# Shorter tile choice on VectorE, two small steps moved to POOL and ACT, unbroken moves of the probabilities and a new issue order, in a fused attention and top-1 mixture-of-experts kernel

## The chip, the core and the metric

The kernel runs on one core of a Trainium2 chip. The metric is the device time of one execution in microseconds (us). PE is TensorE, DVE is VectorE, ACT is ScalarE, POOL is GpSimd, and SP is the engine whose queue issues most DMAs.

## The reference

Four batches of 12288 queries of width 128 attend to 768 pooled keys, which serve as values too. Each of the 49152 resulting rows then goes through the one expert (of eight) that its logits favour.

```python
kv_pool = kv.reshape(B, H // r, r, W // r, r, C).mean(axis=(2, 4))
k = v = kv_pool.reshape(B, -1, C) @ w_sr
s = scale * (q @ k.transpose(0, 2, 1))
a = np.exp(s - s.max(-1, keepdims=True))
a /= a.sum(-1, keepdims=True) + 1e-09
x = (a @ v).reshape(B * S, D)
logits = x @ w_gate
expert_idx = np.argmax(logits, axis=1)
probs = np.exp(logits - logits.max(-1, keepdims=True))
probs /= probs.sum(-1, keepdims=True) + 1e-09
gate_w = probs[np.arange(N), expert_idx]
out[mask] = gate_w[mask, None] * (np.maximum(x[mask] @ w1[e], 0.0) @ w2[e])
```

## The kernel before

The queries are cut into 96 blocks of 512 rows (four groups g of 128), and one block is one round of a software pipeline. A value is kept as a high part in the matmul's own format and a low part that is the rest, so that each product takes three matmuls (`mm3`, L229 to L232: high by high, high weight by low data, low weight by high data). ACT makes the high part with a copy (`high`, L215) and DVE or POOL subtracts it to get the low part (`low`, L218).

One round holds pieces of several blocks at different stages. For the block that is in attention: `turn_q`, `high_q` and `low_q` turn and split the queries (`ql` is subtracted on POOL); `scores` are 24 matmuls of 128x384; `maxima` (L341, DVE) and `exps` (L349, ACT) make the probabilities; `turn_p` (L358, DVE) turns them in blocks of 32x32 into `pb`; `move_p` (L368) brings the blocks to their partitions in `pt` with 16 DMAs from SP's queue; `high_p` and `low_p` split `pt` into `pth` (ACT) and `pt` (POOL), in three pieces n; `values` are 18 matmuls; `copy_x` copies the result out. `route` follows. `turn_x` (L484) multiplies by the identity and the gate's weights at once; DVE makes logits, the one-hot `oh` and its counts `tot`; `gate` ends in L555, and `norm_row` (L502, ACT, four instructions) scales the rows by it into `row`; `ranks` (L559, L560) are two small matmuls that count rows; `places` adds positions up (DVE, then POOL, L570 and L571); `put` (L579) scatters the rows to the expert's list `xs` in DRAM with four indirect DMAs that POOL issues. `row` also gets a token number and padding, which POOL writes (L470, L471) for a later block.

For the tile of 512 rows that is in an expert: `choose` (L639) picks the tile's expert in small DVE steps of width 8 that run one behind the other; `weights` fetches new weights; `read` loads the rows as `xb`; `turn_m`, `high_m` and `low_m` make `xt`, `xh` and `xl` (`xl` is subtracted on DVE); `first` and `second` are 48 matmuls of 128x512, with `hh` (L808, ACT) and `hlow` (L812, DVE) between them; `copy_y` (L830, ACT) takes the sum out as `yt`, `turn_y` (L835, PE) turns it, `rows_y` (L841, ACT) copies it, and `put` (L846) scatters it to the output with four indirect DMAs of POOL.

PSUM has eight banks. Three of them go round in a list (`take` takes the oldest free one, `give` returns it): `first`, `ranks`, `turn_y` and the second part of `turn_x` take theirs from it, so a taker waits for whoever last read the bank. The first six blocks turn their probabilities with PE and move nothing.

The order of PE, ACT and DVE is written out by hand: each step is put at a time of a plan, in units of which a round has 16, and the table `AT` holds these times. Each engine runs its steps in the order of those times and waits at a step until its inputs are there. POOL's and SP's orders are made by the scheduler of the language.

Of the kernel before, what the change touches and what calls it, by code (L numbers as in the profile page):

```python
# [10 lines left out]
F32 = mybir.dt.float32  # L11
F32R = mybir.dt.float32r
# [4 lines left out]
ALU = mybir.AluOpType  # L17
# [4 lines left out]
P = 128  # L22
# [10 lines left out]
    "turn_q": -0.15, "high_q": 3.96, "low_q": 4.25, "maxima": 1.13, "exps": 2.45, ("first_p", 0): 6.32,  # L33
    ("first_p", 1): 4.1, ("first_p", 2): 5.9, ("first_p", 3): 5.1, ("first_p", 4): 5.32,
    ("first_p", 5): 7.4, "first_high": 0.5, "first_low": 1.3, "first_values": 2.0, "turn_p": 2.65,
    "move_p": 16.3, ("high_p", 0): 26.62, ("high_p", 1): 28.22, ("high_p", 2): 29.02, "low_p": 0.8,
    ("values", 0): 37.6, ("values", 1): 38.01, ("values", 2): 39.41, ("values", 3): 40.11,
    ("values", 4): 41.61, ("values", 5): 42.21, "copy_x": 0.6, "turn_x": 1.76, "logits": 0.8, "row": 0.9,
    "gate_exp": 2.27, "gate": 2.29, "ranks": 1.12, "places": 1.21, "put_x": 3.7, "expert": 24.43,
    "fetch": -11.4, "read": -9.0, "weights": -5.41, ("cut", 0, 0): -5.5, ("cut", 1, 0): 3.67,  # L40
    ("cut", 0, 1): 1.39, ("cut", 1, 1): 3.0, "turn_m": -4.26, "high_m": 0.26, "low_m": 2.94, "first": 4.65,
    "high_h": 0.0, "low_h": 1.35, "second": 4.85, "copy_y": 0.42, "turn_y": 1.5, "rows_y": 4.66,
# [20 lines left out]
def tile_pooled_attention_top1_moe(ctx: ExitStack, tc, q, kv, w_sr, w_gate, w1, w2, out):  # L63
# [150 lines left out]
    def high(dst, src):  # L214
        nc.scalar.copy(out=dst, in_=src)  # L215
# [95 lines left out]
    def attention(t, i):  # L311
# [43 lines left out]
        def turn_p(g):  # L355
            if g == 0:
                own["pb"] = ap.tile([P, NK // SQ, G, SQ], F32, name="pb")
            nc.vector.transpose(  # L358
                out=own["pb"][:, :, g, :], in_=own["prob", g].rearrange("p (k t) -> p k t", t=SQ)
            )  # L360

        def move_p():
            pt = own["pt"] = ap.tile([P, NB, T], F32R, name="pt")
            src = own["pb"].rearrange("p (k c) g t -> p c k (g t)", c=QT)
            dst = pt.bitcast(F32).rearrange("p k (a t) -> p a k t", a=QT)
            for a in range(QT):
                for c in range(QT):
                    nc.sync.dma_start(  # L368
                        out=dst[c * SQ : (c + 1) * SQ, a], in_=src[a * SQ : (a + 1) * SQ, c]
                    )  # L370

        def high_p(n):
            own["pth", n] = ap.tile([P, 2, T], F32R, name="pth", bufs=4)
            high(own["pth", n], own["pt"][:, 2 * n : 2 * n + 2].bitcast(F32))

        def low_p(n):
            v = own["pt"][:, 2 * n : 2 * n + 2]
            low(v, v.bitcast(F32), own["pth", n], nc.gpsimd)


        def turn_first(n):
            if n == 0:
                own["pt"] = ap.tile([P, NB, T], F32R, name="pt").rearrange("p n t -> p (n t)")
                own["pb"] = ap.tile([P, NK // SQ, G, SQ], F32, name="pb").rearrange("p n g t -> p (n g t)").bitcast(F32R)
# [15 lines left out]
        def values(k):  # L400
# [3 lines left out]
            if i < FIRST:  # L404
                ph, pl = (own[x].rearrange("p (g b t) -> p g b t", g=G, b=NB)[:, :, k, :] for x in ("pt", "pb"))
            else:
                ph, pl = own["pth", k // 2][:, k % 2], own["pt"][:, k]
# [52 lines left out]
    state["rows"] = count0  # L460
    state["puts"] = []

    def route(t, i, own):
        def norm():
            sums = own["sum"] = table("sum", G, 3)
            nc.vector.tensor_scalar_add(sums, own["sums"], 1e-9)
# [78 lines left out]
        def gate(n):  # L545
            if n == 0:
                own["se"] = rp.tile([P, G], F32, name="se")
# [66 lines left out]

    order = table("order", E, 1)
# [4 lines left out]
    def prefer(tag, last, held, base):  # L620
# [3 lines left out]
            out=pri, in0=last, scalar=float(E), in1=wdesc, op0=ALU.mult, op1=ALU.add  # L624
# [14 lines left out]
    def choose(j):  # L639
# [46 lines left out]
        with nc.allow_low_precision("row numbers below 2**24 are exact"):  # L686
            nc.vector.reduce_sum(out=num, in_=pks, axis=AX.X)
        state["some"] = some
# [4 lines left out]
            out=nheld, in0=state["held"][j % 2], scalar=none, in1=pick, op0=ALU.mult, op1=ALU.add  # L693
# [74 lines left out]
    def experts(t, j):  # L768
# [133 lines left out]
    nc.vector.tensor_copy(out=more, in_=state["some"])  # L902
# [31 lines left out]
```

## Time and profile before

| what | value |
|---|---|
| time, median of 3 runs | 2428.05 us (2422.09 to 2429.71) |
| profiled execution, its own time | 2419.68 us |
| profiled execution, its span | 2417.9 us |
| PE busy | 2166.5 us (90%) |
| DVE busy | 1873.8 us (77%) |
| POOL busy | 1706.7 us (71%) |
| ACT busy | 1469.0 us (61%) |
| mean share of 16 DMA engines, from 300 to 2150 us | 0.65 |

The profiled execution is one run with the profiler on; its time is its span and 1.8 us around it, and it lies 8.4 us under the median of the runs. Busy shares are averages over a filling stage, a long steady stage and a draining stage. PE's busy time counts overlapping matmuls once, and their ends are modelled. In a row of waits the first name is who waited, the second is whose work ended the wait.

### The profile page before, as it was taken

The page shows a single profiled execution, that of the slowest core. Times are in us where ns is not written, and L with a number is a line of the kernel's source. Part 1 is how long each engine was busy: PE and PEld are TensorE (multiplying, and loading weights), DVE is VectorE, ACT ScalarE, POOL GpSimd, SP SyncE. Part 2 cuts the span into 40 slices and gives each one's busy share as a digit, 9 for nine tenths or more (in the row PEclk, how much of TensorE's full clock was granted, in tenths as well). Part 3 has the DMA queues.
Part 4 walks back from the last instruction along what each step waited for, and adds up shares of the span by engine and source line. Part 5 has one row for each costly group of instructions (what it writes and reads, how often), then busy time and mean ns, then how long its engine had stood idle before and what let it go on. Part 6 is the DMA issues. An engine that isn't in the chain of part 4 may idle for free.

```text
span 2417.9 us, 41081 instructions
## 1 busy us (share of the span) xinstructions
PE 2166.5 (90%) x10444; PEld 1803.9 (75%) x10444; DVE 1873.8 (77%) x4883; ACT 1469.0 (61%) x2935; POOL 1706.7 (71%) x1855
## 2 busy tenths in 40 slices
PE   4779999999999999999998999999998999999875
PEld 3667777787777777778777777777777777778665
DVE  6566879988777788988777788997877778788564
ACT  2656666666666666666665666666665666666443
POOL 2645777777767777777767777777767777777643
PEclk9889999999999999999999999999999999999997
DMA  8866667756576567766566566776666565565342
GB/s 238 279 176 139 123 126 153 162 114 120 110 178 121 117 116 158 158 120 124 115 146 143 117 122 138 157 142 119 117 144 151 109 124 112 116 124 106 78 104 52
DMA packets 820757, 324.57 MB, mean 134 GB/s; under 512 B 497048, under 2 KB 792089, under 8 KB 818464
## 3 DMA queue, kind: packets, MB, share of 16 engines
q1 hardware_dynamic: 795808, 268.34, 56.5%
q0 software_dynamic: 24704, 53.53, 6.6%
q8 instruction: 85, 1.39, 0.3%
q14 instruction: 160, 1.31, 0.2%
HBM read 287.84 MB, written 72.88 MB: 149 GB/s over the span
## 4 chain that ended last, share of the span: by engine, by line
PE 52%; issue 10%; ACT 9%; DVE 9%; POOL 8%; DMA 6%; SPq 5%; another core or an unknown queue 0%; ACTq 0%; POOLq 0%; DVEq 0%
PE ps L232 17%; PE ps L230 16%; PE ps L231 15%; SPq L368 4%; POOL pt L218 4%; DVE pb L358 3%; ACT row L502 3%; PE ps L484 3%; ACT hh L808 2%; POOL out_dram L846 2%; PE ps L835 2%; DMA xs<-row,dst 2%; ACT prob L349 2%; DMA pt<-pb 1%; ACT yt L830 1%
## 5 line engine op out<-in xcount | busy, mean ns | idle before, releaser
L808 ACT ACTIVATE hh<-ps 128x512 fp32r<-128x512 f32 x776 | 468.7, 604 | 508.2 <-PE ps L232 379.5
L812 DVE SCALAR_TENSOR_TENSOR hlow<-ps,hh 128x512 fp32r<-128x512 f32 x776 | 527.0, 679 | 165.9 <-ACT hh L808 108.4
L218 POOL TENSOR_TENSOR pt<-pt,pth 128x1024 fp32r<-128x1024 f32 x270 | 638.2, 2403 | 8.6 <-ACT pth L215 7.7
L846 POOL DMA_INDIRECT out_dram<-yo,tok x388 | 386.2, 995 | 155.2 <-issue 111.4
L579 POOL DMA_INDIRECT xs<-row,dst x384 | 377.4, 983 | 116.7 <-issue 93.7
L341 DVE TENSOR_REDUCE nmax<-ps 128x1 f32<-128x768 f32 x384 | 364.6, 950 | 81.3 <-PE ps L232 60.6
L349 ACT ACTIVATE prob<-ps,nmax 128x768 f32<-128x768 f32 x384 | 346.5, 902 | 117.8 <-DVE nmax L341 55.3
L358 DVE STREAM_TRANSPOSE pb<-prob 128x768 f32<-128x768 f32 x360 | 350.9, 975 | 62.9 <-ACT prob L349 42.6
L230 PE MATMUL ps<-xh,wt 128*128 128x512 f32 (+1 forms) x800 | 328.5, 411 | 58.5 <-DVE hlow L812 44.0
L230 PE MATMUL ps<-hh,wt 128*128 128x512 f32 (+1 forms) x800 | 324.2, 405 | 0.0
L231 PE MATMUL ps<-hlow,wt 128*128 128x512 f32 (+1 forms) x800 | 314.7, 393 | 3.4 <-DVE hlow L812 3.1
L231 PE MATMUL ps<-xl,wt 128*128 128x512 f32 (+1 forms) x800 | 315.0, 394 | 0.0
L232 PE MATMUL ps<-xh,wt 128*128 128x512 f32 (+1 forms) x800 | 313.7, 392 | 0.0
L232 PE MATMUL ps<-hh,wt 128*128 128x512 f32 (+1 forms) x800 | 313.2, 392 | 0.0
L230 PE MATMUL ps<-kh,qh 128*128 128x384 f32 x768 | 272.6, 355 | 30.4 <-ACT prob L349 27.3
L215 ACT CAST pth<-pt 128x1024 fp32r<-128x1024 f32 x270 | 274.1, 1056 | 0.0
L232 PE MATMUL ps<-kh,ql 128*128 128x384 f32 x768 | 263.5, 343 | 0.4 <-POOL ql L218 0.4
L231 PE MATMUL ps<-kl,qh 128*128 128x384 f32 x768 | 262.1, 341 | 0.0
L230 PEld LDWEIGHTS ps<-xh,wt 128*128 128x128 f32 x800 | 153.7, 192 | 91.3 <-DVE hlow L812 52.3
L232 PE MATMUL ps<-pth,vl 128*128 128x512 f32 x540 | 213.6, 395 | 0.0
L231 PE MATMUL ps<-pt,vh 128*128 128x512 f32 x540 | 211.4, 392 | 0.0
L230 PE MATMUL ps<-pth,vh 128*128 128x512 f32 x540 | 210.8, 390 | 0.0
(131 smaller groups left out, 3792.1 us busy)
## 6 DMA issues: line engine op xcount, KB each, us to landing
wt<-ws SPq DMA_DIRECT2D x94, 2048.0 KB
pt<-pb SPq DMA_DIRECT2D x1440, 96.0 KB
raw<-in_kv_dram SPq DMA_DIRECT2D x96, 256.0 KB
qb<-in_q_dram SPq DMA_DIRECT2D x384, 64.0 KB
xb<-xs SPq DMA_DIRECT2D x376, 64.0 KB
ws<-wt SPq DMA_DIRECT2D x8, 2048.0 KB
raw<-in_moe_w_dram SPq DMA_DIRECT2D x16, 512.0 KB
out_dram<-yo,tok POOLq DMA_INDIRECT x388
```

Of the source, the lines that this page charges most:

```text
L215: nc.scalar.copy(out=dst, in_=src)
L218: eng.tensor_tensor(out=dst, in0=src, in1=h.bitcast(F32), op=ALU.subtract)
L230: nc.tensor.matmul(out=ps, lhsT=wh, rhs=xh, start=start, stop=False)
L231: nc.tensor.matmul(out=ps, lhsT=wh, rhs=xl, start=False, stop=False)
L232: nc.tensor.matmul(out=ps, lhsT=wl, rhs=xh, start=False, stop=stop)
L341: nc.vector.tensor_reduce(out=nmax, in_=own["s", g][:, :, :NH], op=ALU.max, axis=AX.XY, negate=True)
L349: nc.scalar.activation(out=prob.rearrange("p (h k) -> p h k", h=2), in_=own["s", g][:, :, :NH], func=AF.Exp, bias=own["nmax", g], scale=1. ...
L358: nc.vector.transpose(out=own["pb"][:, :, g, :], in_=own["prob", g].rearrange("p (k t) -> p k t", t=SQ))
L579: put = nc.gpsimd.indirect_dma_start(out=xs, out_offset=bass.IndirectOffsetOnAxis(ap=dst[:, g : g + 1].bitcast(U32), axis=0), in_=own["row ...
L808: nc.scalar.activation(out=hh, in_=own["hp", f], func=AF.Relu)
L812: nc.vector.scalar_tensor_tensor(out=hl, in0=own["hp", f], scalar=0.0, in1=own["hh", f].bitcast(F32), op0=ALU.max, op1=ALU.subtract,)
L846: put = nc.gpsimd.indirect_dma_start(out=out, out_offset=bass.IndirectOffsetOnAxis(ap=own["tok"][:, g : g + 1].bitcast(U32), axis=0), in_= ...
```

## The change

Five things change, and with them the order.

- `choose` takes fewer DVE steps. The priorities are scaled below one, so that "has enough rows" plus priority is one instruction, and a constant column of 0.5 beside it (`av` is twice as wide, and the maximum is taken over nine columns) makes `top` over 1 mean that there is a tile. `some` and `none` (L659, L660) go, and one of the two steps L649 and L653.
- `low_m` subtracts `xl` on POOL.
- The step on the probabilities' sums (L466) moves from DVE to ACT; `se` moves to PSUM.
- `pb` and `pt` change their layout, so that each of the 16 moves copies one run of 768 numbers in a partition instead of six runs of 128. The number of moves and their bytes stay.
- The table `AT` gets new times. `norm_row` goes behind `ranks`.

```diff
-    "turn_q": -0.15, "high_q": 3.96, "low_q": 4.25, "maxima": 1.13, "exps": 2.45, ("first_p", 0): 6.32,
+    "turn_q": -0.15, "high_q": 3.34, "low_q": 5.01, "maxima": 1.13, "exps": 2.45, ("first_p", 0): 5.48,
...
-                own["pb"] = ap.tile([P, NK // SQ, G, SQ], F32, name="pb")
+                own["pb"] = ap.tile([P, QT, NB, G, SQ], F32, name="pb")
...
-            pt = own["pt"] = ap.tile([P, NB, T], F32R, name="pt")
-            src = own["pb"].rearrange("p (k c) g t -> p c k (g t)", c=QT)
-            dst = pt.bitcast(F32).rearrange("p k (a t) -> p a k t", a=QT)
+            pt = own["pt"] = ap.tile([P, QT, NB, P], F32R, name="pt")
+            src = own["pb"].rearrange("p c b g t -> p c (b g t)")
+            dst = pt.bitcast(F32).rearrange("p a b t -> p a (b t)")
...
-            sums = own["sum"] = table("sum", G, 3)
-            nc.vector.tensor_scalar_add(sums, own["sums"], 1e-9)
+            sums = own["sum"] = rp.tile([P, G], F32, name="sum", bufs=3)
+            nc.scalar.activation(out=sums, in_=own["sums"], func=AF.Identity, bias=tiny, scale=1.0)
...
-        av = table("av", E)
-        nc.vector.tensor_scalar(
-            out=av, in0=rem, scalar1=0.5 if final else T - 0.5, scalar2=4.0 * E, op0=ALU.is_gt, op1=ALU.mult
+        av = table("av", 2 * E)
+        nc.vector.scalar_tensor_tensor(
+            out=av[:, :E], in0=rem, scalar=0.5 if final else T - 0.5, in1=pri, op0=ALU.is_gt, op1=ALU.add
         )
         yield
-        nc.vector.tensor_tensor(out=av, in0=av, in1=pri, op=ALU.add)
+        top = rp.tile([P, 1], F32, name="top" + tag)
+        nc.vector.reduce_max(out=top, in_=av[:, : E + 1], axis=AX.X)
         yield
-        top = rp.tile([P, 1], F32, name="top" + tag)
-        nc.vector.reduce_max(out=top, in_=av, axis=AX.X)
-        yield
-        some, none = (rp.tile([P, 1], F32, name=x + tag) for x in ("some", "none"))
-        nc.vector.tensor_scalar(out=some, in0=top, scalar1=4.0 * E, scalar2=None, op0=ALU.is_ge)
-        nc.vector.tensor_scalar(out=none, in0=top, scalar1=4.0 * E, scalar2=None, op0=ALU.is_lt)
-        yield
+
         pick = rp.tile([P, E], F32, name="pick" + tag)
-        nc.vector.tensor_scalar(
-            out=pick, in0=av, scalar1=top, scalar2=some, op0=ALU.is_equal, op1=ALU.mult
-        )
+        nc.vector.tensor_scalar(out=pick, in0=av[:, :E], scalar1=top, scalar2=None, op0=ALU.is_equal)
...
-            low(own["xl"], own["xt"], own["xh"], nc.vector)
+            low(own["xl"], own["xt"], own["xh"], nc.gpsimd)
```

What the new order does shows at three places of a round. The first is PE's queue around the ranks (`tot` and `upper`) and the turning of the finished tile (`yt`), before:

```order
L232 MATMUL ps<-xh,wt_109 128x512
L559 LDWEIGHTS upper
L559 MATMUL ps<-tot,upper 128x8
L560 LDWEIGHTS ones
L560 MATMUL ps<-tot,ones 128x8
L835 MATMUL ps<-ident,yt 128x128 x4
L230 MATMUL ps<-hh,wt_109 128x512
```

And with the change:

```order
L232 MATMUL ps<-xh,wt_109 128x512
L562 LDWEIGHTS upper
L562 MATMUL ps<-tot,upper 128x8
L563 LDWEIGHTS ones
L563 MATMUL ps<-tot,ones 128x8
L230 MATMUL ps<-hh,wt_109 128x512
L231 MATMUL ps<-hlow,wt_109 128x512
L232 MATMUL ps<-hh,wt_109 128x512
L835 MATMUL ps<-ident,yt 128x128 x4
```

The turning of the finished tile now stands behind three matmuls of `second`. The second place is ACT's queue, from the copy of a block's result to the next piece of `pth`, before:

```order
L543 ACTIVATE ex<-df 128x32
L808 ACTIVATE hh<-ps 128x512
L502 ACTIVATE row<-ps,gate 128x128 x4
L830 COPY yt<-ps 128x512
L808 ACTIVATE hh<-ps 128x512
...
L841 COPY yo<-ps 128x512
L808 ACTIVATE hh<-ps 128x512 x2
L349 ACTIVATE prob,sums<-ps,nmax 128x768
L215 CAST pth<-pt 128x1024
L416 COPY xt<-ps 128x512
```

And with the change:

```order
L546 ACTIVATE ex<-df 128x32
L808 ACTIVATE hh<-ps 128x512
L830 COPY yt<-ps 128x512
L505 ACTIVATE row<-ps,gate 128x128 x4
L808 ACTIVATE hh<-ps 128x512
...
L841 COPY yo<-ps 128x512
L808 ACTIVATE hh<-ps 128x512
L215 CAST pth<-pt 128x1024
L808 ACTIVATE hh<-ps 128x512
L349 ACTIVATE prob,sums<-ps,nmax 128x768
L417 COPY xt<-ps 128x512
```

The four scalings of rows change places with the copy of the finished tile, and the first piece of `pth` goes two instructions forward. The third place is a whole round of POOL's queue, from one scatter of rows to the next, before:

```order
L579 DMA xs<-row,dst 397312x144 x4
L470 MEMSET row 128x4x15
L471 TENSOR_SCALAR row<-slot 128x4
L789 CAST tok<-tokf 128x4
L846 DMA out_dram<-yo,tok 49152x128 x4
L218 TENSOR_TENSOR pt<-pt,pth 128x1024 x3
L570 TENSOR_TENSOR pos<-pos,oh 128x8 x3
L571 TENSOR_TENSOR pos<-pos,oh 128x32
L218 TENSOR_TENSOR ql<-qt,qh 128x512
L579 DMA xs<-row,dst 397312x144 x4
```

And with the change:

```order
L582 DMA xs<-row,dst 397312x144 x4
L218 TENSOR_TENSOR xl<-xt,xh 128x512
L473 MEMSET row 128x4x15
L474 TENSOR_SCALAR row<-slot 128x4
L846 DMA out_dram<-yo,tok 49152x128 x4
L218 TENSOR_TENSOR pt<-pt,pth 128x4x256 x3
L573 TENSOR_TENSOR pos<-pos,oh 128x8 x3
L574 TENSOR_TENSOR pos<-pos,oh 128x32
L218 TENSOR_TENSOR ql<-qt,qh 128x512
L789 CAST tok<-tokf 128x4
L582 DMA xs<-row,dst 397312x144 x4
```

The scheduler puts `xl` between the scatter and the MEMSET of `row` in 66 of the 84 rounds of this kind; in the other 18, in which a new batch's keys are made, it stands behind the MEMSET and L474.

## Rows read from the trace of the kernel before

**Rows 1.** Windows: length, busy us of PE, PEld, DVE, ACT, POOL (instructions), clock, DMA.

```profile
300.00:2150.00 1850.00, 1723.21 (x8308) 1432.58 (x8307) 1503.46 (x3884) 1172.83 (x2346) 1389.52 (x1502) 1.00 0.65 132
```

**Rows 2.** Waits, 300 to 2150 us: total us, times, longest.

```profile
POOL row L470 <- DMA xs<-row,dst: 172.2, 79, 6.4
ACT row L502 <- DVE gate L555: 68.3, 75, 1.3
POOL ql L218 <- ACT qh L215: 62.7, 60, 1.7
PE ps L559 <- ACT row L502: 43.9, 74, 0.9
PE ps L230 <- ACT prob L349: 25.7, 50, 1.5
PE ps L835 <- ACT yt L830: 21.5, 75, 0.3
PE ps L230 <- DVE hlow L812: 21.3, 21, 3.3
```

**Rows 3.** One line, L416: count, ns min/median/max, first and last start.

```profile
L416 ACT COPY xt<-ps x90: 575/589/597, 213.3 to 2289.1; 128x512 f32<-128x512 f32 x90
```

**Rows 4.** Lines of POOL, 300 to 2150 us: busy us, mean ns, idle before.

```profile
L218 POOL TENSOR_TENSOR pt<-pt,pth 128x1024 fp32r<-128x1024 f32 x237 | 560.4, 2404 | 0.8
L218 POOL TENSOR_TENSOR ql<-qt,qh 128x512 fp32r<-128x512 f32 x79 | 101.7, 1287 | 62.9 <-ACT qh L215 62.7
```

**Rows 5.** Lines of DVE, 300 to 2150 us.

```profile
L218 DVE TENSOR_TENSOR xl<-xt,xh 128x512 fp32r<-128x512 f32 x80 | 52.4, 655 | 0.0
L653 DVE TENSOR_TENSOR ps<-ps,pri 128x8 f32<-128x8 f32 x79 | 13.7, 174 | 2.7
L466 DVE TENSOR_SCALAR ps<-sums 128x4 f32<-128x4 f32 x79 | 11.9, 151 | 0.0
L660 DVE TENSOR_SCALAR none<-top 128x1 f32<-128x1 f32 x79 | 11.0, 139 | 0.0
L659 DVE TENSOR_SCALAR some<-top 128x1 f32<-128x1 f32 x79 | 8.7, 110 | 0.0
```

**Rows 6.** Timeline of PE around one round's ranks: start us, us, instruction, idle before.

```profile
1014.02 0.40 PE L232 MATMUL ps<-xh,wt 128*128 128x512 f32 x1
1015.06 0.17 PE L559 MATMUL ps<-tot,upper 128*128 128x8 bf16 x1 [0.65 <-ACT row L502]
...
1015.54 0.66 PE L835 MATMUL ps<-ident,yt 128*128 128x128 f32 x4 [0.29 <-ACT yt L830]
```

**Rows 7.** Timeline of DVE and ACT, the same microseconds.

```profile
1013.66 0.17 DVE L555 RECIPROCAL gate<-se 128x4 f32<-128x4 f32 x1
1013.78 0.22 DVE L539 TENSOR_REDUCE tot<-oh 128x8 bf16<-128x32 f32 x1
...
1013.87 1.14 ACT L502 ACTIVATE row<-ps,gate 128x128 f32<-128x128 f32 x4 [0.91 <-DVE gate L555]
1014.88 0.60 ACT L830 COPY yt<-ps 128x512 f32<-128x512 f32 x1
```

**Rows 8.** Timeline of POOL, behind the next scatter of rows.

```profile
1028.40 0.15 POOL L470 MEMSET row<- 128x60 f32 x1 [3.10 <-DMA xs<-row,dst]
```

**Rows 9.** Timeline of ACT, ahead of the pieces of pth.

```profile
1021.74 0.60 ACT L808 ACTIVATE hh<-ps 128x512 fp32r<-128x512 f32 x1 [1.17 <-issue]
...
1024.51 0.60 ACT L808 ACTIVATE hh<-ps 128x512 fp32r<-128x512 f32 x1 [0.48 <-issue]
1028.36 0.60 ACT L808 ACTIVATE hh<-ps 128x512 fp32r<-128x512 f32 x1 [3.26 <-PE ps L232]
...
1029.73 1.05 ACT L215 CAST pth<-pt 128x1024 fp32r<-128x1024 f32 x1
```

**Rows 10.** Timeline of SP, the last of 16 moves.

```profile
1023.84 0.62 SPq L368 DMA_DIRECT2D pt<-pb  x1
```

**Rows 11.** The chain that ended last: start us, us; one move from issue to landing.

```profile
1013.76 3.46 DMA pt<-pb
```

More of the change, by code (lines that the diff above doesn't have):

```diff
@@ L32 @@
 AT = {
-    "turn_q": -0.15, "high_q": 3.96, "low_q": 4.25, "maxima": 1.13, "exps": 2.45, ("first_p", 0): 6.32,
[L34 to L42, printed above, removed]
+    "turn_q": -0.15, "high_q": 3.34, "low_q": 5.01, "maxima": 1.13, "exps": 2.45, ("first_p", 0): 5.48,
+    ("first_p", 1): 4.1, ("first_p", 2): 4.74, ("first_p", 3): 5.1, ("first_p", 4): 5.32,
+    ("first_p", 5): 7.4, "first_high": 0.5, "first_low": 1.3, "first_values": 2.69, "turn_p": 2.65,
+    "move_p": 17.32, ("high_p", 0): 28.78, ("high_p", 1): 25.01, ("high_p", 2): 29.02, "low_p": 0.45,
+    ("values", 0): 37.6, ("values", 1): 38.01, ("values", 2): 39.41, ("values", 3): 39.91,
+    ("values", 4): 41.61, ("values", 5): 42.21, "copy_x": 0.6, "turn_x": 1.76, "logits": 0.8, "row": 1.7,
+    "gate_exp": 2.27, "gate": 2.29, "ranks": 1.12, "places": 2.13, "put_x": 3.83, "expert": 24.43,
+    "fetch": -12.69, "read": -9.0, "weights": -5.6, ("cut", 0, 0): -7.93, ("cut", 1, 0): 3.67,
+    ("cut", 0, 1): 1.14, ("cut", 1, 1): 3.1, "turn_m": -4.57, "high_m": 1.58, "low_m": 2.94, "first": 4.6,
+    "high_h": 0.0, "low_h": 1.35, "second": 4.85, "copy_y": 0.52, "turn_y": 1.61, "rows_y": 4.66,
 }
@@ L356, in turn_p @@
             if g == 0:
[L357 removed]
+                own["pb"] = ap.tile([P, QT, NB, G, SQ], F32, name="pb")
             nc.vector.transpose(
[L359 removed]
+                out=own["pb"][:, :, :, g, :].rearrange("p c b t -> p b c t"),
+                in_=own["prob", g].rearrange("p (b c t) -> p b c t", c=QT, t=SQ),
             )
         def move_p():
[L363 to L365 removed]
+            pt = own["pt"] = ap.tile([P, QT, NB, P], F32R, name="pt")
+            src = own["pb"].rearrange("p c b g t -> p c (b g t)")
+            dst = pt.bitcast(F32).rearrange("p a b t -> p a (b t)")
             for a in range(QT):
@@ L372, in high_p @@
         def high_p(n):
-            own["pth", n] = ap.tile([P, 2, T], F32R, name="pth", bufs=4)
-            high(own["pth", n], own["pt"][:, 2 * n : 2 * n + 2].bitcast(F32))
+            own["pth", n] = ap.tile([P, QT, 2, P], F32R, name="pth", bufs=4)
+            high(own["pth", n], own["pt"][:, :, 2 * n : 2 * n + 2].bitcast(F32))
         def low_p(n):
-            v = own["pt"][:, 2 * n : 2 * n + 2]
+            v = own["pt"][:, :, 2 * n : 2 * n + 2]
             low(v, v.bitcast(F32), own["pth", n], nc.gpsimd)
@@ L382, in turn_first @@
             if n == 0:
-                own["pt"] = ap.tile([P, NB, T], F32R, name="pt").rearrange("p n t -> p (n t)")
-                own["pb"] = ap.tile([P, NK // SQ, G, SQ], F32, name="pb").rearrange("p n g t -> p (n g t)").bitcast(F32R)
+                own["pt"] = ap.tile([P, QT, NB, P], F32R, name="pt").rearrange("p a b t -> p (a b t)")
+                own["pb"] = ap.tile([P, QT, NB, G, SQ], F32, name="pb").rearrange("p c b g t -> p (c b g t)").bitcast(F32R)
             pp = own["pp", n] = take()
@@ L406, in values @@
             else:
-                ph, pl = own["pth", k // 2][:, k % 2], own["pt"][:, k]
+                ph, pl = own["pth", k // 2][:, :, k % 2], own["pt"][:, :, k]
             mm3(own["xa"], vh[:, k], vl[:, k], ph, pl, k == 0, k == NB - 1)
@@ L460, in tile_pooled_attention_top1_moe @@
     state["rows"] = count0
+    tiny = cp.tile([P, 1], F32, name="tiny")
+    nc.gpsimd.memset(tiny, 1e-9)
     state["puts"] = []
@@ L546, in gate @@
             if n == 0:
-                own["se"] = rp.tile([P, G], F32, name="se")
+                own["se"] = table("se", G)
                 nc.vector.reduce_sum(out=own["se"], in_=own["ex"], axis=AX.X)
@@ L613, in tile_pooled_attention_top1_moe @@
     state["held"] = [zero, zero]
+    for n in range(2):
+        nc.vector.memset(table("av", 2 * E)[:, E:], 0.5)
+    wfrac = cp.tile([P, E], F32, name="wfrac")
+    nc.gpsimd.tensor_scalar(out=wfrac, in0=wdesc, scalar1=1.0 / (8 * E), scalar2=None, op0=ALU.mult)
     order = table("order", E, 1)
@@ L623, in prefer @@
         nc.vector.scalar_tensor_tensor(
-            out=pri, in0=last, scalar=float(E), in1=wdesc, op0=ALU.mult, op1=ALU.add
+            out=pri, in0=last, scalar=0.125, in1=wfrac, op0=ALU.mult, op1=ALU.add
         )
@@ L687, in choose @@
             nc.vector.reduce_sum(out=num, in_=pks, axis=AX.X)
-        state["some"] = some
+        state["top"] = top
         state["tile", j] = {"num": num, "thr": thr}
@@ L692, in choose @@
         nc.vector.scalar_tensor_tensor(
-            out=nheld, in0=state["held"][j % 2], scalar=none, in1=pick, op0=ALU.mult, op1=ALU.add
+            out=nheld, in0=state["held"][j % 2], scalar=top, in1=pick, op0=ALU.is_gt, op1=ALU.add
         )
@@ L901, in tile_pooled_attention_top1_moe @@
     more = rp.tile([P, 1], I32, name="more")
-    nc.vector.tensor_copy(out=more, in_=state["some"])
+    nc.vector.tensor_scalar(out=more, in0=state["top"], scalar1=1.0, scalar2=None, op0=ALU.is_ge)
     go = nc.values_load(more[0:1, 0:1], min_val=0, max_val=1)
```

## The prediction

> **What bounds the kernel now.** I read the windows first, to find the stage that is worth something. From 300 to 2150 us the kernel runs 79 rounds (the 79 `ql` of [rows 4]) in 1850 us, 23.42 us each, at full clock [rows 1]. PE is idle for 1850 - 1723.2 = 127 us of that, 1.6 us a round, so no engine is simply full. Next I read the waits of that stretch [rows 2] and asked which of them PE feels. Four groups make 112 of the 127 us: the ranks wait for ACT's scaled rows (43.9), the turning of the finished tile waits for ACT's copy `yt` (21.5), scores wait for the exponentials (25.7), and `first` waits for `hlow` to free a bank (21.3).
>
> The first two are one chain, and the timelines show it. DVE has `tot`, all that the ranks need, at 1013.78 + 0.22 = 1014.00, and PE issued its last matmul at 1014.02. Yet the ranks start at 1015.06, just after ACT's four scalings end at 1013.87 + 1.14 = 1015.01 [rows 6, 7]: the ranks take the bank that these scalings still read. The copy `yt` stands behind the scalings and ends at 1015.48, and the turning starts at 1015.54. The scalings themselves waited for `gate` [rows 2].
>
> Then I asked how much room the other engines leave, and POOL is the surprise. It is busy for 75% of the stretch, but its queue is almost closed. Of its waits, the longest (172.2 us, 2.18 a round) is its own doing: the MEMSET of `row` waits until the scatter that POOL itself has just issued has landed, 3.10 us in the round shown [rows 2, 8]. Only the wait of `ql` for `qh`, 62.7 / 79 = 0.79 us a round, is for somebody else. So POOL alone would need 23.42 - 0.79 = 22.63 us a round. However much PE's waits shrink, a round falls to about 22.6 us and no further, unless POOL's own queue gets shorter.
>
> **The change part by part.**
>
> *Ranks, rows and `yt`.* With the rows behind the ranks, the ranks take a bank that ACT's scalings don't hold and wait for `tot` alone; `yt` goes ahead of the scalings, and the turning goes behind three matmuls. At most this gives (43.9 + 21.5) / 79 = 0.83 us a round; at the least nothing, if the wait only changes its name. I take all of it, since `tot` ends 1.0 us before the scalings do [rows 7]. What is late next is `hlow` and the exponentials, which keep 0.6 us a round.
>
> *Steps off DVE.* `some` and `none` (0.110 and 0.139), one of two steps of 0.174, the sums' term (0.151) and `xl` (0.655) leave: 1.23 us of DVE a round [rows 5]. DVE is 81% busy [rows 1], so most of this only lengthens its idle time. On the path lies at most PE's wait for `hlow`, 21.3 / 79 = 0.27 us, and at the least nothing; I take half, 0.13. The sums' term costs ACT less than an `hh` of 0.60 us [rows 9]; ACT is 63% busy and gets it between two `hh`, so I cost it at nothing, and that cover is gone only if ACT sits on the path there.
>
> *`xl` on POOL.* The row of the same shape on POOL is `ql`: 1.287 us against 0.655 on DVE [rows 4, 5]. In 66 of 84 rounds `xl` stands between the scatter and the MEMSET, that is, inside the 2.18 us in which POOL only waits for the landing. There it costs nothing, and POOL's own round stays at 22.63. In the other 18 it stands behind the MEMSET and POOL needs up to 22.63 + 1.29 = 23.92 us, more than today's mean round; I give these rounds no gain at all.
> The Trainium skill, GPSIMD Engine Reference, section 4.1, speaks against this edit: it wants elementwise work on VectorE, because GpSimd is about twice as slow with two inputs. The trace agrees on the ratio (1287 / 655 = 1.97). Followed as a rule, it gives the last rival below.
>
> *Unbroken moves.* Number and bytes stay; six runs become one. The trace has no such move. Bounds: the issue costs the same 0.62 us each [rows 10], and nothing is gained; or landings get quicker by all that POOL waits beyond `xl`, 2.18 - 1.29 = 0.89 us a round. I take nothing: `pth` is ready in time already, and what else delays the scatter's landing is not in a row. The new layout also makes POOL's `low_p` read four runs of 256. At most that costs as if each piece were two instructions of 512, 2 x 1287 - 2404 = 170 ns, three times a round, 0.51 us [rows 4]; at the least nothing. I take nothing, since it stays one instruction of the same size.
>
> *New order.* The first piece of `pth` goes two instructions forward, to where ACT now waits 3.26 us for PE. Its moves are issued until 1023.84, and a move lands at most 3.46 us later in the row I have, at 1027.30 [rows 9 to 11]; with 1.05 for the piece that ends at 1028.35, just as the next `hh` starts (1028.36). So it fits, with nothing to spare at the late end. I charge 0.10 us a round for such meetings. `tok` only changes its place. In the filling and draining stages I count nothing: there the waits are for data from far back.
>
> *Sum.* PE's side offers 0.83 + 0.13 = 0.96 us a round, POOL's queue allows 0.79; the smaller decides, less 0.10: 0.69. There are 89 rounds between the first and last of 90 copies [rows 3]; 66/84 of them, 70, gain. 70 x 0.69 = 48 us. The profiled execution took 2419.68 us (its span 2417.9 and 1.8 around it), so 2419.7 - 48 = 2372. That execution lies 8.4 us under the median of the runs shown; on the runs' scale I say 2380. If half of the ranks' wait stays (0.28 us), or the four runs of 256 cost a third of their bound, 70 x 0.45 = 31 us is left, 2397; with nothing charged and 0.8 in all 89 rounds it is 2357. The forecast's own range is 2355 to 2400.
>
> **The rivals.**
>
> *POOL's queue gets shorter too.* If landings become quicker by 0.3 us or more, POOL no longer caps the round, and PE's side comes through whole: 0.83 + 0.27 = 1.10 in 89 rounds, 98 us, 2330. For it: the landing wait differs much from round to round (mean 2.18, longest 6.4 [rows 2]), so something delays it. Against it: nothing shows that it is the moves.
>
> *The early piece of `pth` blocks ACT.* If the moves land at the late end and the round is 0.7 us shorter, `hh` and the exponentials behind the piece start 0.7 us late in each round, and PE waits for them: the gain is given back, 2428, no change. For it: the fit above is exact. Against it: 3.46 us was one landing that the chain picked, and such are late ones.
>
> *POOL becomes the bound.* `xl` at the head of POOL's queue waits for `xh`, which ACT now makes one `hh` later; behind it wait the MEMSET, both scatters and all of `low_p`. Then it is not hidden in any round: 22.63 + 1.29 = 23.92 instead of 23.42, 0.50 x 89 = 44 us more, 2472. It decides from the point where more than 0.79 us of `xl` stays uncovered. Against it: `xh` would end near 1021.74 + 0.60 + 0.62 = 1022.96, POOL is free at 1028.40 - 3.10 = 1025.30 [rows 8, 9], so ACT would have to slip by 2.3 us. This is where the skill's rule on VectorE would lead, and the place in the queue is what speaks against it.
>
> **How the numbers follow.** About 0.3%, 7 us, is what a measurement of this kernel can tell from no change. The forecast has a chance of 0.60, the shorter queue 0.20, ACT's block 0.10, POOL as the bound 0.10. Faster is 0.60 + 0.20 = 0.80, same 0.10, slower 0.10. The range runs from the shorter queue's time less the width of its own terms, 2326, to no change and a little beyond, 2432; it leaves out the slow rival and some of the first.
>
> **What would show it.** Right: PE's waits for `row` and `yt` near zero, the ranks starting within 0.3 us of `tot`; a round of about 22.7 us; the MEMSET's wait cut from 2.18 to about 0.9 with `xl` ahead of it; `ql`'s wait for `qh` gone, and DVE now and then waiting for POOL's `pos`. Wrong: `xl` waiting for `xh`; the first `pth` waiting for moves with `hh` late behind it; a `low_p` much over 2.40 us; or a round under 22.4 us, which would say that POOL's queue was not the cap.

## The result, and the profile after

The kernel before took 2422.09 us in these runs (median of 9, 2418.48 to 2431.68), the changed one 2403.45 (median of 9, 2387.87 to 2410.69). The ratio is 0.9901 with a 95% interval of 0.9875 to 0.9927: faster by 1.0%, some 24 us (the two medians alone differ by 18.6 us, the two profiled executions by 15.8). 48 us were forecast. The direction held, and 2403 us lies in the stated range of 2326 to 2432, but just outside the 2355 to 2400 that the forecast gave itself. Half of the gain is missing, and it is missing just where the forecast was made. The profiled execution of the changed kernel took 2403.92 us (span 2402.1).

First the place of the gain. This is the row of `copy_x` on ACT (L417), one start a round; it answers to [rows 3].

```profile
L417 ACT COPY xt<-ps x90: 577/586/587, 211.8 to 2281.9; 128x512 f32<-128x512 f32 x90
```

89 rounds take 2281.9 - 211.8 = 2070.1 us, 23.26 each; before, they took 2289.1 - 213.3 = 2075.8, 23.32 each. So the rounds, for which 48 us were forecast, gave 5.7 us. The stage behind the last copy gave more, though nothing was counted there: 2417.9 - 2289.1 = 128.8 us before, 2402.1 - 2281.9 = 120.2 now. The start gave 1.5. These three are the 15.8 us between the two profiled executions.

Then the stretch from 300 to 2150 us again: the window (columns as in [rows 1]: busy time of PE, PE's weight loads, DVE, ACT and POOL, clock, DMA share, GB/s), and the waits (total us, times, longest), which answer to [rows 2]. Here and below, lists of waits show some rows of a longer list, in its order.

```profile
300.00:2150.00 1850.00, 1718.32 (x8328) 1430.84 (x8327) 1448.87 (x3490) 1207.87 (x2431) 1496.40 (x1585) 1.00 0.57 132
```

```profile
PE ps L562 <- DVE hlow L812: 88.5, 75, 1.3
POOL row L473 <- DMA xs<-row,dst: 75.5, 62, 5.1
POOL ql L218 <- ACT qh L215: 60.4, 56, 1.3
ACT pth L215 <- DMA pt<-pb: 54.8, 39, 3.0
DVE dst L580 <- POOL pos L574: 22.0, 12, 4.2
...
PE ps L230 <- DVE hlow L812: 18.6, 23, 2.2
PE ps L230 <- ACT prob L349: 14.6, 32, 1.3
```

The turning of the finished tile no longer waits for `yt`, as forecast. The ranks (now L562) no longer wait for ACT's scaled rows, as forecast. But they wait all the same, and longer: 88.5 us in place of 43.9, now for DVE's `hlow` (L812). PE is idle for 1850 - 1718.3 = 132 us, 5 more than before. The timeline of one round shows the step (start in us, duration, engine, line, operation; in brackets the engine's idle time before it and what ended it):

```profile
1129.14 0.21 DVE L542 TENSOR_REDUCE tot<-oh 128x8 bf16<-128x32 f32 x1
1129.23 1.14 ACT L505 ACTIVATE row<-ps,gate 128x128 f32<-128x128 f32 x4 [0.79 <-DVE gate L558]
...
1129.35 0.71 DVE L320 STREAM_TRANSPOSE qt<-qb 128x512 f32<-128x512 f32 x1
1129.99 0.65 DVE L812 SCALAR_TENSOR_TENSOR hlow<-ps,hh 128x512 fp32r<-128x512 f32 x1
...
1130.69 0.17 PE L562 MATMUL ps<-tot,upper 128*128 128x8 bf16 x1 [1.26 <-DVE hlow L812]
```

`tot` ends at 1129.35. The ranks start at 1130.69, 0.05 us after `hlow` has ended. They have nothing to do with `hlow`: they take the next bank that comes free, and that is the one which `hlow` still reads. `hlow` stands behind `qt`, 0.71 us, in DVE's queue. Before, the bank that came free was the one that ACT's scalings read.

POOL's groups, which answer to [rows 4] and [rows 8] (busy us, mean ns, idle before):

```profile
L218 POOL TENSOR_TENSOR pt<-pt,pth 128x1024 fp32r<-128x1024 f32 x237 | 560.2, 2404 | 0.8
...
L218 POOL TENSOR_TENSOR xl<-xt,xh 128x512 fp32r<-128x512 f32 x80 | 104.6, 1307 | 1.0
L218 POOL TENSOR_TENSOR ql<-qt,qh 128x512 fp32r<-128x512 f32 x79 | 101.7, 1288 | 60.8 <-ACT qh L215 60.4
```

`xl` costs 1.31 us, and almost all of it is hidden: the MEMSET's wait for the landing falls from 172.2 to 75.5 us, by 97 of `xl`'s 105. `low_p` on four runs of 256 takes 2.404 us, as before to the nanosecond.

### The profile page after: what moved, and what is told of

The parts are those of the page before. It is cut to its first block, busy times and chain, and to the rows that moved or that the text cites. A ratio compares the mean times of both kernels' runs of the same rounds, so it can differ in the third digit from the quotient of the medians.

```text
span 2402.1 us, 40694 instructions
## 1 busy us (share of the span) xinstructions
PE 2153.1 (90%) x10444; PEld 1794.4 (75%) x10444; DVE 1801.2 (75%) x4386; ACT 1505.7 (63%) x3031; POOL 1833.3 (76%) x1957
## 4 chain that ended last, share of the span: by engine, by line
PE 60%; issue 12%; DVE 11%; POOL 5%; ACT 5%; DMA 3%; SPq 2%; DVEq 0%; ACTq 0%; POOLq 0%; another core or an unknown queue 0%
PE ps L232 19%; PE ps L230 18%; PE ps L231 18%; DVE hlow L812 3%; PE ps L487 3%; DVE qt L320 2%; ACT hh L808 2%; POOL pt L218 2%; ACT prob L349 2%; PE ps L835 2%; POOL out_dram L846 1%; SPq L369 1%; DMA xs<-row,dst 1%; DVE pb L358 1%; ACT pth L215 1%
## 5 line engine op out<-in xcount | busy, mean ns | idle before, releaser
L218 POOL TENSOR_TENSOR pt<-pt,pth 128x1024 fp32r<-128x1024 f32 x270 | 638.1, 2404 | 2.2 <-ACT pth L215 1.3
L812 DVE SCALAR_TENSOR_TENSOR hlow<-ps,hh 128x512 fp32r<-128x512 f32 x776 | 528.1, 680 | 142.6 <-ACT hh L808 99.6
L218 POOL TENSOR_TENSOR ql<-qt,qh 128x512 fp32r<-128x512 f32 x96 | 123.7, 1289 | 112.2 <-ACT qh L215 111.7
```

The costliest lines, as they stand in the source:

```text
L218: eng.tensor_tensor(out=dst, in0=src, in1=h.bitcast(F32), op=ALU.subtract)
L812: nc.vector.scalar_tensor_tensor(out=hl, in0=own["hp", f], scalar=0.0, in1=own["hh", f].bitcast(F32), op0=ALU.max, op1=ALU.subtract,)
```

## The experiments

They ran in four groups, each on one chip: 1 to 4, 5 to 8, 9 to 11, and 12. There the kernel before takes 2377 to 2384 us, in place of 2422. The chip of the two kernels above is not on record; it is called the first chip here, since it is most likely another one. Every ratio is to the kernel before on the same chip; two ratios of one group compare more safely than two of different groups. "Ordinary" is a round of at most 24.5 us, measured from one start of `copy_x` to the next.

**1. The ranks in a place of their own**, in the PSUM bank that `table` keeps for small lists, so that they take no bank from the common stock.

```diff
-            rk = own["rk"] = take()
+            rk = own["rk"] = table("rk", 2 * E)
...
-            give(rk)
```

> The changed kernel, but the ranks write 16 columns of the bank that holds the small tables, and take no bank from the list. Theory A (the ranks now wait for the bank that hlow still reads, and hlow stands behind the turning of the queries on DVE): PE's wait at the ranks falls from 88.5 us in 300 to 2150 us to under 25, a round from 23.36 to about 22.7 us (POOL's own queue needs 22.6), some 55 us less in all, near 2345. Rival B (the wait only moves on, to second or to the scores, because DVE itself is late): PE's idle time in the stretch stays near 130 us and the time within 0.3% of the changed kernel's 2403.

2343.07 us, ratio 0.9832 [0.9814, 0.9851]. No wait of the ranks for `hlow` is left. What is late next, in the waits from 300 to 2150 us:

```profile
POOL row L473 <- DMA xs<-row,dst: 87.0, 68, 4.8
DVE dst L579 <- POOL pos L573: 79.7, 59, 4.1
...
PE ps L230 <- DVE hlow L811: 50.3, 50, 5.6
...
POOL ql L218 <- ACT qh L215: 2.9, 6, 0.8
```

POOL waits for little but its own scatter, and DVE waits for POOL's `pos`. Theory A had the wait right and the gain too large: it named 55 us less than the changed kernel, and by the ratios (0.9832 here, 0.9927 in experiment 5) it is 1.0%, some 23 us. Part of the wait moved on, as its rival had said: `first` waits 50.3 us for `hlow`, where the changed kernel waits 21.6 (experiment 5). One taker less also changes who gets which bank.

**2. `qt` behind `hlow`.** The same wait taken away from the other end.

```diff
-    "turn_q": -0.15, "high_q": 3.34, "low_q": 5.01,
+    "turn_q": 0.75, "high_q": 2.44, "low_q": 4.11,
```

> The changed kernel with the turning of the queries (qt, 0.71 us on DVE) one place later, behind the hlow whose bank the ranks take; their high and low parts stay where they are. Theory A: the ranks start about 0.65 us earlier, their wait falls from 88.5 to about 37 us, a round by 0.4 to 0.6 us, time 2350 to 2370. Rival B: the maxima that now stand behind qt become late by the same 0.7 us, and the time is within 0.3% of 2403.

2353.68 us, ratio 0.9866 [0.9846, 0.9885]. The waits of the same stretch:

```profile
DVE dst L580 <- POOL pos L574: 60.6, 47, 4.4
PE ps L562 <- DVE hlow L812: 29.7, 81, 0.9
```

The ranks still wait for `hlow`, in each of 81 rounds, but only 0.37 us. The two edits have nothing in common but this wait, and both show that the bank was what held the ranks. The gain over the changed kernel is 0.6% here.

**3. The unbroken moves alone**, on the kernel before (the layout of `pb` and `pt`, `move_p`, `high_p` and `low_p` of the change).

> The kernel before with nothing but the unbroken moves (layouts of pb and pt). Theory A (moves are hidden): POOL's wait for its scatter to land, 172 us in the stretch, falls by less than a fifth, and the time is within 0.3% of the kernel before. Rival C (the moves delay the landings and pth): that wait falls by 40 us or more and the time by 0.5% or more, which would make the moves the source of the measured 1%.

2380.64 us, ratio 0.9990 [0.9973, 1.0007]: nothing. The MEMSET waits as long as ever:

```profile
POOL row L471 <- DMA xs<-row,dst: 188.0, 79, 7.1
```

So the landing of the scatter isn't held up by the moves, and the rival "POOL's queue gets shorter" has no cause. 0 was the right value of that term.

**4. All parts, old order.** The changed kernel with the table `AT` of before.

> The changed kernel with the table of times of the kernel before: all parts of the change but the order. Theory A (the order's gain at the ranks and the turning was given back, so the order is worth little): within 0.5% of the changed kernel, 2395 to 2415. Rival D (the order carries the 1%, the parts alone are worth nothing): within 0.3% of the kernel before, 2415 to 2430.

2445.38 us, ratio 1.0263 [1.0242, 1.0284]. Neither expectation allowed for this. With the old order `xl` stands behind the MEMSET, where the wait for the landing doesn't hide it:

```profile
POOL row L473 <- DMA xs<-row,dst: 183.4, 78, 6.9
DVE dst L580 <- POOL pos L574: 103.7, 60, 4.0
PE ps L562 <- ACT row L505: 60.1, 77, 1.1
```

The round takes 23.73 us on average, 0.71 more than in experiment 3, and POOL's `ql` waits only 16.6 us for `qh`, so POOL's queue is closed. This is the third rival, "not hidden in any round", as a real case: the old order takes away what the prediction named against it, the place in the queue. That its 23.92 us lie so near is luck: they were added up on the first chip, where ordinary rounds are half a microsecond longer. No run has the other parts in the old order with `xl` on DVE, so the share of `xl` in this loss is argued.

**5. The changed kernel again**, beside 6, 7 and 8.

> The changed kernel, unaltered, timed beside the kernel before and beside the next three, so that all ratios share one baseline. Theory A (the ranks' wait only moved from ACT's scalings to DVE's hlow): ratio to before 0.990 again, within 0.004, and PE again idle for about 88 us of 1850 before the ranks with hlow as what ended it; then the ranks' own bank (0.983) and qt behind hlow (0.987) are gains over the changed kernel itself. Rival: the chip of those two runs was simply kinder to the new order: ratio 0.983 to 0.987 for the unaltered kernel too, and the two edits bought nothing.

2355.93 us, ratio 0.9927 [0.9911, 0.9943], and the waits as on the first chip:

```profile
PE ps L562 <- DVE hlow L812: 82.4, 81, 1.2
ACT pth L215 <- DMA pt<-pb: 75.1, 60, 2.9
...
PE ps L230 <- DVE hlow L812: 21.6, 24, 2.2
...
POOL ql L218 <- ACT qh L215: 7.8, 19, 1.1
```

So by the ratios experiments 1 and 2 are gains over the changed kernel and no gift of their chip. The clearest number is the ordinary round: 22.56 us here, 22.60 in experiment 3, which has the old order (first chip: 23.07 after, 23.10 before). The wait changed its name and did not get shorter. One wait isn't as on the first chip: `ql` waits 7.8 us for `qh`, not 60.4. Here POOL's queue is nearly closed in the changed kernel too.

**6. A third buffer for `row`** on top of experiment 1, so that the MEMSET needn't wait for the scatter just issued.

```diff
-            row = own["row"] = rp.tile([P, G, W], F32, name="row")
+            row = own["row"] = rp.tile([P, G, W], F32, name="row", bufs=3)
```

> The ranks in a bank place of their own, and a third buffer for row, so that POOL's MEMSET waits for the scatter of the round before and not for the one just issued. Theory B (with the ranks free POOL's queue is the cap, 22.6 us a round, 1.1 of it the MEMSET's wait for the landing): that wait goes to nearly nothing, the round shortens by 0.5 to 1.0 us until PE and the exponentials bind, and the ratio to before goes from 0.983 to 0.945 to 0.970. Rival (POOL's queue looks closed only because it waits for the same thing as everybody; PE's own work and its waits for the exponentials are the cap): the MEMSET's wait goes too, but it comes back as a wait of ql for qh or of pos for the ranks, and the ratio stays within 0.980 to 0.986.

2340.74 us, ratio 0.9865 [0.9848, 0.9882]; in microseconds that is experiment 1 again, and beside experiment 5 on the same chip it is 0.6% less (15 us). The edit missed its aim:

```profile
POOL row L473 <- DMA xs<-row,dst: 87.3, 66, 5.1
```

The MEMSET was simply issued one round earlier, again right behind the scatter that frees the buffer. This says nothing on POOL's cap; experiments 11 and 12 do.

**7. The ten-step choice alone**, on the kernel before.

> The kernel before with the ten-step choice of tiles alone (xl, the sums' term, the rows, the moves and the order as before). If the choice is what shortened the stage behind the last copy (128.8 to 120.2 us), this kernel has about 120 us there too, while the round stays as before: 8 to 10 us less, ratio 0.996 (0.994 to 0.998). If the two or three steps of DVE a round also lie on PE's path, up to 0.13 us a round more, ratio 0.991 to 0.993. Rival (the drain got shorter by the new order or by xl on POOL): about 128 us there, ratio 0.998 to 1.001.

2397.50 us, ratio 1.0099 [1.0082, 1.0117]: slower, which neither side expected. The last stage takes 116.9 us, so the gain there is the choice's. The loss lies in the rounds: five of them take 28.7 to 30.4 us. The next experiment shows what made two of these long.

**8. `xl` back on DVE**, all else as in the changed kernel.

> The changed kernel with xl back on DVE and all else kept, the new order too. If xl's 0.655 us of DVE a round was on PE's path (qt and hlow stand behind it and the ranks wait for hlow), the changed kernel's gain of 24 us is mostly this edit's: up to 0.655 x 84 = 55 us slower than the changed kernel, ratio to before about 1.00 to 1.012. If DVE's idle quarter covers it, ratio 0.988 to 0.992 as for the changed kernel, POOL's MEMSET waits 2.1 us a round again, and xl on POOL was neither cost nor gain.

2374.09 us, ratio 0.9998 [0.9981, 1.0015]. By the time alone, `xl` would lie on the path. But the ordinary rounds are as short as in 5, and two take 30.4 and 30.6 us. One of these, first POOL, then DVE:

```profile
1517.04 0.97 POOL L846 DMA_INDIRECT out_dram<-yo,tok  x1 [0.30 <-issue]
1518.03 6.99 POOL L218 TENSOR_TENSOR pt<-pt,pth 128x1024 fp32r<-128x1024 f32 x3
```

```profile
1517.62 7.55 DVE L257 TENSOR_TENSOR pooled<-half 128x128 f32<-128x128 f32 x1
1525.10 0.68 DVE L812 SCALAR_TENSOR_TENSOR hlow<-ps,hh 128x512 fp32r<-128x512 f32 x1
```

`pooled <- half` is the sum of two halves of the next batch's keys; it takes 0.25 us when it runs alone. Here it took 7.55: by the record it started 0.41 us before POOL's three `pt`, and it ended 0.15 us after the last of them. The profile of 7 has two such holds (7.43 and 7.23 us), those of 1 and 3 one each (7.73 and 7.08), the changed kernel's two profiles none. Over all profiles from 200 us on, 25 of these sums were held: each started while a `pt` ran or at most 0.57 us before the first. The other 173 ran in about 0.25 us, with the next `pt` at least 0.65 us away. The Trainium skill, SBUF — State Buffer, section "Who interferes with whom", says that a VectorE instruction with two inputs in SBUF contends with a GpSimd instruction that reads SBUF. The trace agrees, and shows more: all but one of the 25 holds lasted until the last of three `pt` standing one behind the other had ended, not over one of 2.40 us. (The other one, in experiment 4, ended behind the first `pt`, after 2.24 us.)

**9. `xl` on DVE, without the hold.** Kernel 8, with the sum left to PE, which turns both halves into the same place in PSUM.

```diff
-            nc.tensor.transpose(out=pt[:, :P], in_=own["pooled", kb], identity=ident)
+            for h in range(2):
+                nc.tensor.matmul(out=pt[:, :P], lhsT=own["half", kb, h], rhs=ident, start=h == 0, stop=h == 1)
...
```

> The run with xl back on DVE again, but the sum of two halves (pooled <- half, L257) is left to PE, which adds them in PSUM while it turns them. In that run's profile this DVE instruction took 7.55 and 7.72 us in two rounds instead of 0.25, each time held until POOL's three pt instructions behind one another had ended. Theory C (these two holds, 15 us, are what that run lost against the changed kernel, and xl on DVE costs nothing by itself): ratio to before 0.991 to 0.9945, as the changed kernel's 0.9927, and no round near 30 us. Rival (xl's 0.65 us a round lies on the path, or its own meetings with POOL do): 0.998 to 1.001 again, with 22.3 us rounds made longer throughout.

2350.33 us, ratio 0.9865 [0.9843, 0.9887]: better than theory C asked for, and by its ratio at least as good as the changed kernel (0.9927, in another group). No round is near 30 us, while the MEMSET waits 179.0 us again. So the move of `xl` to POOL shows no gain for itself: it is hidden there, and it is hidden on DVE. What the sum on PE costs or gains besides was not tried on the changed kernel.

**10. The choice alone, without the hold**: kernel 7 with the same edit.

> The ten-step choice alone on the kernel before, which was 1.0% slower than before, again with the sum of two halves left to PE. Its profile had two such holds of DVE, 7.43 and 7.23 us. Theory C (two to three holds make the loss, and the choice saves about 6 us behind the last copy): ratio 0.996 to 1.003. Rival (the shorter choice itself makes rounds longer, since DVE's steps now fall so that dst waits for POOL's pos): 1.006 to 1.011 with no round near 30 us.

2385.58 us, ratio 1.0010 [0.9996, 1.0024]. Without the sum on DVE the loss of 1.0% is gone, so it was the holds. The last stage takes 119.4 us, yet nothing is left of it in the total: `dst` waits 106.5 us for `pos` here, against 71.5 in experiment 3.

**11. No MEMSET**, on top of experiment 1.

```diff
+    kept = [cp.tile([P, G, W], F32, name="kept%d" % n) for n in range(2)]
+    for row in kept:
+        nc.gpsimd.memset(row[:, :, P + 1 :], 0.0)
+    slots = iota("slots", NS * G, P, 0, 1)
...
-            row = own["row"] = rp.tile([P, G, W], F32, name="row")
-            nc.gpsimd.memset(row[:, :, P + 1 :], 0.0)
-            nc.gpsimd.tensor_scalar(
-                out=row[:, :, P], in0=slot, scalar1=float(i * T), scalar2=None, op0=ALU.add
-            )
+            own["row"] = kept[i % 2]
...
+                nc.vector.scalar_tensor_tensor(
+                    out=own["row"][:, :, P], in0=own["gate"], scalar=-1.0, in1=slots[:, i * G : (i + 1) * G],
+                    op0=ALU.is_lt, op1=ALU.add,
+                )
```

> The ranks in a place of their own, and row in two lasting buffers whose zero columns are filled once at the start; the slot numbers are written by one small DVE step behind gate, from a list made at the start, so POOL has no MEMSET, no slot step and no wait for a landing in a round. This removes 1.1 us of wait and 0.38 us of work from POOL's queue, which the third buffer did not do (there the MEMSET was issued a round earlier and stood behind the scatter again). Theory B (POOL's queue is the cap once the ranks are free): the six in seven ordinary rounds go from 21.6 to 22.3 us down to 21.0 to 21.4, and the ratio to before from 0.983 to 0.95 to 0.97. Rival (PE's own work of 21.2 to 21.6 us a round is the cap): the ordinary rounds settle at 21.6 without the scatter up to 22.3, ratio 0.975 to 0.982, and POOL now waits for qh, pth or pos instead. If DVE's extra step of 0.17 us is on the path: 0.984 to 0.99.

2581.25 us, ratio 1.0833 [1.0810, 1.0855]. Two small steps of DVE cost over 200 us: the new one of 128x4 numbers, and the sum of the halves. Their groups on DVE, the window of the stretch (columns as above), then a round's timeline, first POOL, then DVE:

```profile
L559 DVE SCALAR_TENSOR_TENSOR kept<-gate,slots 128x4 f32<-128x4 f32 x72 | 128.3, 1782 | 3.0 <-DVE gate L558 0.6
L257 DVE TENSOR_TENSOR pooled<-half 128x128 f32<-128x128 f32 x18 | 118.8, 6602 | 0.0
```

```profile
300.00:2150.00 1850.00, 1628.53 (x7598) 1342.37 (x7597) 1559.82 (x3264) 1101.06 (x2217) 1337.47 (x1298) 0.96 0.52 122
```

```profile
1193.86 4.64 POOL L218 TENSOR_TENSOR pt<-pt,pth 128x1024 fp32r<-128x1024 f32 x2
```

```profile
1193.94 0.17 DVE L558 RECIPROCAL gate<-ps 128x4 f32<-128x4 f32 x1
1194.14 4.38 DVE L559 SCALAR_TENSOR_TENSOR kept<-gate,slots 128x4 f32<-128x4 f32 x1
1198.45 0.19 DVE L542 TENSOR_REDUCE tot<-oh 128x8 bf16<-128x32 f32 x1
```

`gate` and `slots` both lie in SBUF, and in three rounds of four (54 of the 72 in the stretch) the step is held by POOL's `pt`. `gate` itself, with its input in PSUM, ran in 0.17 us beside the same `pt`. `tot` and the ranks stand behind the held step. The sum of the halves is held in all of its 18 rounds, 6.19 to 7.52 us each: with POOL's queue shifted, it now meets `pt` every time. Against 0.17 and 0.25 us the two lose 116 and 114 us of DVE's time in the stretch. The granted clock is 0.96 there, where it is 1.00 in experiment 1; what that adds to the 8% was not measured.

**12. The same, with one input in PSUM.** The step reads `se` in place of `gate`, and the sum of the halves is left to PE as in 9.

```diff
-                    out=own["row"][:, :, P], in0=own["gate"], scalar=-1.0, in1=slots[:, i * G : (i + 1) * G],
+                    out=own["row"][:, :, P], in0=own["se"], scalar=-1.0, in1=slots[:, i * G : (i + 1) * G],
```

> The kernel with the ranks in a place of their own and no MEMSET once more, with two edits: the new slot step on DVE reads the PSUM list se in place of gate, so that only one of its inputs lies in SBUF (with two it took 1.78 us on average in the run before, at most 4.38, and ended each time just behind a pt of POOL; beside no pt it took 0.17), and the sum of two halves is left to PE, so that no step of DVE in these rounds but the few of the choice has two SBUF inputs. Theory D (the 8% were these holds alone): the step takes 0.16 to 0.2 us, no round near 30 us, and the ratio is below 1 by 1.5% or more. Theory B on top of it (POOL's queue was the cap at 0.983): ordinary rounds of 21.0 to 21.5 us, ratio 0.955 to 0.975. Rival to B (PE's own work is the cap): ordinary rounds at 21.6 without scatter, ratio 0.975 to 0.985. Rival to D (the lasting buffers themselves cost, since the scatter's issue or ACT's scalings now wait for landings): ratio 1.0 or more with a step of 0.17 us.

2295.08 us, ratio 0.9627 [0.9613, 0.9642]: 3.7% faster than before and the best of all. The step, the window and the waits of the stretch:

```profile
L555 DVE SCALAR_TENSOR_TENSOR kept<-ps,slots 128x4 f32<-128x4 f32 x83 | 12.3, 148 | 0.5 <-issue 0.5
```

```profile
300.00:2150.00 1850.00, 1808.53 (x8775) 1491.27 (x8774) 1513.79 (x3727) 1250.70 (x2543) 1540.14 (x1494) 1.00 0.59 137
```

```profile
POOL ql L218 <- ACT qh L215: 55.5, 79, 1.2
POOL pos L572 <- DVE pos L570: 46.9, 34, 2.4
...
PE ps L230 <- DVE hlow L811: 8.6, 18, 0.5
PE ps L230 <- DMA wt<-ws: 8.2, 5, 1.9
```

148 ns against 1782 for the same step in the same place: theory D holds for the two steps together. PE is idle for 41.5 us of 1850 (132 in the changed kernel), and POOL waits for others again. From 0.983 to 0.963 is at most what POOL's queue had still cost once the ranks were free: the two edits were not tried apart, and a hold of 7.5 us in experiment 1's profile is part of it. Theory B's ratio came true, but its 21.0 to 21.5 us for an ordinary round didn't: the commonest value is 21.6 to 21.8 (27 of 89 rounds, 15 lie below), near what its rival had named for PE's own work. Experiment 1 has 20 rounds at that value too; the gain lies in the others. With PE busy for 98% of the stretch, little is left to take from its waits.

## Why the prediction was right in direction and wrong in size

- **The range.** It held because it reached to "no change and a little beyond". The forecast's own range did not, and by its sum it should have ended lower still: with half of the ranks' wait left, 0.96 - 0.28 - 0.10 = 0.58 us a round and 2387; with a third of the four runs' bound, 0.52 and 2392; not 0.45 and 2397.
- **Ranks, rows, `yt` (0.83 us a round).** The failed step is "the ranks take a bank that ACT's scalings don't hold and wait for `tot` alone". It gave a lower bound, "nothing, if the wait only changes its name", and dropped it because `tot` ends 1.0 us before the scalings. That reason looked at one holder of a bank. There was a second, `hlow`, already in [rows 2] as what `first` waits for, and no part of the change was aimed at it. The ranks wait 88.5 us for it, where they had waited 43.9. Experiments 1 and 2 free the ranks, and by the ratios (0.9832 and 0.9866 beside 0.9927) gain 1.0% and 0.6% over the changed kernel; experiment 6, beside it on one chip, gains 0.6%. That is 15 to 23 us for a wait of 1.0 us a round (82.4 us in 81 rounds of experiment 5), which over 89 rounds is 91. So the bank is shown to hold the ranks, but to take a wait of PE for time, as the 0.83 did, was a second fault: most of it moves on.
- **DVE's steps (0.13).** They left, DVE's busy time in the stretch fell from 1503 to 1449 us, and neither the choice alone (experiment 10) nor `xl`'s engine (experiment 9) shows a gain by it. The bound below, nothing, fits. The sums' term was not run alone.
- **`xl` on POOL (0).** Right, in cost and in mechanism: with the new order it is hidden (experiments 5 and 9). With the old one a round gets 0.71 us longer where the rival had 0.50, most likely by `xl` (experiment 4).
- **POOL's cap (22.63 us).** Right in kind, not in size. On the first chip the changed kernel doesn't reach it, and `ql`'s wait for `qh` stays at 60.4 us where it was to vanish. Experiment 12 shows that POOL's queue costs time once the ranks are free. But rounds go below 22.4 us, the prediction's own sign against the cap: 51 of the 89 rounds of experiment 5 take 22.2 to 22.4, and the commonest of experiment 1 take 21.6 to 21.8. The wait for the landing, which the cap counts in full, isn't a fixed cost.
- **Unbroken moves and `low_p` (0).** Right: ratio 0.9990, and 2404 ns.
- **The early `pth` (0.10).** It waits for the moves, 54.8 us, as the second rival had it. What that costs wasn't tried alone.
- **First and last stage (nothing).** Wrong by 8.6 us in the last. Before, it took 128.8 us, and 123.7 with the moves alone on another chip; with the new choice it is 116 to 120 in every profile. Experiments 7 and 10, with the choice alone, have 116.9 and 119.4, so some 4 to 7 us are the choice's; the rest isn't explained.
- **What the gain is.** This stays open. Alone, the moves give nothing, the choice nothing in the total, and `xl`'s engine shows nothing. That leaves the new order and the sums' term on ACT, which were not run alone. On the chip of experiment 5 the gain isn't in ordinary rounds: there are fewer long ones (4 above 24.5 us, 9 in experiment 3). On the first chip there are 7 before and 7 after, and 8.6 of the 15.8 us between the two profiles lie in the last stage. So a gain of the right sign came from where none was forecast; the direction was in part luck.

## What to carry to other kernels

When a wait for a recycled buffer is taken away, list all holders of the other buffers with their ends, and count the gain only down to the second latest. Even then, most of a wait may move on to the next taker. Small results that never needed a shared bank are better given a place of their own. Look for a queue that waits for its own transfer: work placed in that wait was free here, and removing the wait was worth more. Keep one input of each small VectorE step in PSUM where GpSimd has long instructions: here a step of 0.25 us took 7.

## What the runs showed of the hardware that was not expected

- **Holds of DVE by POOL**: 0.25 us becomes 7.08 to 7.73 (experiments 1, 3, 7, 8) or 6.19 to 7.52 (experiment 11, every time), 0.17 becomes 1.78 on average (experiment 11), ending 0.03 to 0.16 us behind a `pt`. A shift of a fraction of a microsecond decides whether they happen, and with them 1% of the time (experiments 7 and 10). The mean of a group hides them; its longest instruction shows them.
- **The same kernel differs by 2% between the first chip and the others, and one place stands out.** The changed kernel took 2403 us on the first chip and 2356 in experiment 5, with nearly equal mean durations in its large groups. The first `hh` whose matmuls stand behind the turning of the attention's result (`turn_x`, L487) shows it. On the first chip, PE and then ACT:

```profile
1360.13 0.40 PE L232 MATMUL ps<-xh,wt 128*128 128x512 f32 x1
```

```profile
1361.23 0.60 ACT L808 ACTIVATE hh<-ps 128x512 fp32r<-128x512 f32 x1 [1.50 <-PE ps L232]
```

In experiment 5:

```profile
1336.78 0.40 PE L232 MATMUL ps<-xh,wt 128*128 128x512 f32 x1
```

```profile
1337.27 0.60 ACT L808 ACTIVATE hh<-ps 128x512 fp32r<-128x512 f32 x1 [0.90 <-PE ps L232]
```

`hh` starts 0.70 us after the recorded end of its matmul in the one, 0.09 in the other. In the stretch it is more than 0.2 us late in 58 of 79 rounds on the first chip (50 of 79 in the kernel before), and in at most 4 of some 80 in each of the twelve experiments. At the other `hh` that regularly wait the medians are 0.09 or 0.10 us on both chips. On average it is 0.53 us later than 0.10 on the first chip; over 89 rounds that is 47 us, as much as the two times differ by, but that all of it lies on the path is not shown. The granted clock is 1.00 in both stretches. Matmul ends are modelled, so what made PE's results late on that chip isn't shown and stays open.
